# Places of a batch's rows: a segmented scan on VectorE and two products in place of seven products

## The chip, the cores and the metric

The kernel runs on one core of a Trainium2 chip. The metric is the device time of one execution in microseconds (us). The engines are TensorE (PE; its weight loads are shown as PEld), VectorE (DVE), ScalarE (ACT), GpSimd (POOL) and SyncE (SP, which here issues most of the DMAs). All data are float32.

## The reference

The kernel joins two blocks: an attention in which each query keeps its 32 best keys, and a mixture of experts in which each row goes to one expert.

```python
# attention: q, k, v are (8, 8, 576, 64)
scores = q @ k^T / 8
kth    = the 32nd largest score of each row
attn   = softmax(where(scores >= kth, scores, -1e9))
x      = (attn @ v), laid out as (4608, 512)      # one row per batch and position

# mixture of experts: w_gate (512, 8), w1 (8, 512, 1024), w2 (8, 1024, 512)
logits     = x @ w_gate
expert_idx = argmax(logits, axis=1)
gate_w     = softmax(logits)[row, expert_idx]
perm       = argsort(expert_idx, kind="stable")    # rows sorted by expert
for e in range(8):
    y_sorted[lo:hi] = relu(x_sorted[lo:hi] @ w1[e]) @ w2[e]
out = gate_w[:, None] * y
```

The change concerns the sorting: each row needs its place in a table in HBM (`x_rows`), in which expert e owns the places from e*CAP on, with CAP = 4736, in the order of arrival. A row's place is the first free place of its expert plus the number of earlier rows of the same batch that chose that expert.

## The kernel before

**Stages.** A loop of 144 steps covers 8 batches of 18 steps. Each step searches two tiles of 128 queries by 576 keys for their 32nd largest score. A batch has four units, each a pair of heads. At the end of a batch the gate logits of its 576 rows are complete, the rows get their places and are scattered to `x_rows` by indirect DMAs from GpSimd. From the second batch on, blocks of 128 rows of one expert, which are complete by then, go through the two products of the experts. These blocks are cut into 16 "pieces", which are put between the attention's products on TensorE. After the loop, the last batch is finished, and the remaining blocks run by themselves.

**The order on each engine** is the order in which the program is written, for TensorE, ScalarE and VectorE; nothing rearranges it. Each step of the loop writes:

- VectorE: `fold` (`h`, L315, and `l`, L316, from the scores `s`), `fold_on` (`few`, L322, and `hl`, L330; in the earlier part of the loop `hl` is made by GpSimd, L327 and L328), MAX8 and MATCH_REPLACE8 for the search (L351, L374, L385).
- ScalarE: `low` (L396), two activations `w` (L412), copies of scores from PSUM (`s`, L306), copies `wT` (L445, L447), two exponentials (L429), `wTt` (L462, L464), evacuations of the experts' products (L862, L976, L997).
- GpSimd: two subtractions on `w` (L421), 128x576 each, which wait for the two activations of L412; then `doubt` (L402), `nbias` (L380), scatters (L593) and stores (L880).
- TensorE: transposes `wTm` (L440) of the step before, which `wT` copies; expert pieces (`ph`, L971, and `py`, L988); scores of a later step (L299); output products `po` (L477) and `px` (L488).

Scores are made three steps ahead of their search.

**The end of a batch** is the generator `ending`. It runs over several steps of the loop: at each named place ("products", "small", "relu", "pool" and so on) it goes one stage on. For the sorting the stages are:

- `choice` (L530): five steps on VectorE make `oh`, the one-hot choice of each row (128 rows x 5 tiles x 8 experts), by L538 to L548. Tile 4 has only 64 rows; the upper half of its partitions is kept at zero by `e_same`.
- `ranks` (L554): seven products on TensorE into one PSUM bank `rank`. The first spreads `run`, the first free place of each expert, by the identity; the second multiplies by a triangle (`before`) and counts earlier rows in a tile; the other five multiply by `ones` and add the counts of earlier tiles. Columns 0 to 39 are the places, columns 40 to 47 the new `run`.
- `places` (L566): VectorE multiplies places and choice (L573), adds up (L578) and prepares the gate weights.
- ScalarE copies the new `run` out of PSUM (L1151), and `blocks` (L1153).
- `table` (L623) computes on VectorE, with few elements, which blocks are full (L645 and the lines after it); `filled_up` does so after batch 0, `counted` and `end_table` after the last.

The VectorE steps of `choice`, `places` and `table` don't run in one go. They are put into a list (`aside`), and the search takes one at each "tick". A search has six ticks, one behind each MAX8 and MATCH_REPLACE8 of its third and fourth round; a tick that finds a list at its end goes on to the next list, and does nothing if there is none. What is left of `choice` is taken at the place "turn", and `ranks` comes at "products", both in the following step. In the last batch there are no searches left, and all steps run one after the other.

`k.small` is a pool with two buffers for each name.

Of the kernel before, what the change touches and what calls it, by code (L numbers as in the profile page):

```python
# [9 lines left out]
F32 = mybir.dt.float32  # L10
I32 = mybir.dt.int32
AF = mybir.ActivationFunctionType
# [32 lines left out]
def kernel(  # L45
# [173 lines left out]
    wT = const.tile([P, NC, 2, S + ST], F32, name="wT")  # L219
    doubt = const.tile([P, B * U, NT, NL], F32, name="doubt")  # L220
    nc.gpsimd.memset(doubt, NEG)
    run = const.tile([P, E], F32, name="run")
    prepared.append(lambda: nc.vector.tensor_copy(run, e_at))
    rest_i = const.tile([1, 1], I32, name="rest_i")
    slot_last = const.tile([1, 2, NSLOT + SOON], I32, name="slot_last")
    slot_long = const.tile([1, 3, LONGS], I32, name="slot_long")
# [303 lines left out]
    def choice(lg):  # L530

        r = SimpleNamespace(lg=lg)
        mx = k.small.tile([P, KC], F32, name="mx")
        r.oh = oh = k.small.tile([P, KC, E], F32, name="oh")
        idx = k.small.tile([P, KC], F32, name="idx")

        def steps():
            nc.vector.tensor_reduce(mx, lg, axis=AX.X, op=ALU.max)  # L538
            yield
            nc.vector.tensor_tensor(lg, lg, _inner(mx[:, :], E), op=ALU.subtract)  # L540
            yield
            nc.vector.scalar_tensor_tensor(
                out=oh, in0=lg, scalar=0.0, in1=_ins(e_less[:, :], 1, KC), op0=ALU.is_ge, op1=ALU.mult
            )
            yield
            nc.vector.tensor_reduce(idx, oh, axis=AX.X, op=ALU.min)
            yield
            nc.vector.tensor_tensor(oh, e_same, _inner(idx[:, :], E), op=ALU.is_equal)  # L548
            yield

        r.steps = steps()
        return r

    def ranks(r):  # L554

        rp = bank("rank")
        ohf = r.oh[:, :, :].rearrange("p t e -> p (t e)")
        r.pos, r.run = rp[:, 0:KC * E], rp[:, KC * E:(KC + 1) * E]
        nc.tensor.matmul(rp[:, 0:(KC + 1) * E], ident, _ins(run[:, :], 1, KC + 1), start=True, stop=False)
        nc.tensor.matmul(r.pos, before, ohf, start=False, stop=False)  # L560
        for i in range(1, KC + 1):
            nc.tensor.matmul(
                rp[:, i * E:(KC + 1) * E], ones, ohf[:, 0:(KC + 1 - i) * E], start=False, stop=(i == KC)
            )

    def places(r, x):  # L566

        pos = k.small.tile([P, KC, E], F32, name="pos")
        r.posi = k.small.tile([P, KC], I32, name="posi")
        den = k.small.tile([P, KC], F32, name="den")  # L570

        def steps():
            nc.vector.tensor_tensor(pos, r.pos.rearrange("p (t e) -> p t e", e=E), r.oh, op=ALU.mult)  # L573
            yield
            nc.vector.tensor_reduce(den, r.lg, axis=AX.X, op=ALU.add)
            yield
            with nc.allow_low_precision(reason="one whole number and zeros are added"):
                nc.vector.tensor_reduce(r.posi, pos, axis=AX.X, op=ALU.add)  # L578
            yield
            nc.vector.tensor_scalar_add(den, den, EPS)  # L580
            yield
            nc.vector.reciprocal(x[:, :, Dm], den)
            yield

        return steps()
# [22 lines left out]
    def fill_up():  # L608

        ends = k.small.tile([1, E], I32, name="ends")  # L610
        nc.vector.tensor_copy(ends, run[0:1, :])
        for e in range(E):
            on = nc.gpsimd if e % 2 else nc.sync
            r = on.value_load(ends[0:1, e:e + 1], min_val=e * CAP, max_val=e * CAP + N)
            put = on.dma_start(x_rows[bass.ds(r, P), :], blank).ins
            if not k.exact:
                for other in scattered:
                    tc.add_manual_dep(put, other.name, WAIT)
                for other in fetched:
                    tc.declare_no_dep(put, other, reason="empty rows go behind all full blocks")  # L620
                fills.append(put)

    def table(slot_i, n, last, riding=None):  # L623
# [12 lines left out]
        def steps():  # L636
            if last:
                v.tensor_scalar(full, run[0:1, :], float(P - 1), 1.0 / P, ALU.add, ALU.mult)
                yield
                v.tensor_scalar(full, full, UNDER, WHOLE, ALU.add, ALU.add)  # L640
                yield
                for whole in (full, done):
                    v.tensor_scalar_add(whole, whole, -WHOLE)
            else:
                v.tensor_scalar(full, blocks, WHOLE, None, ALU.add)  # L645
            yield
            if riding is not None:
                v.tensor_tensor(full, full, riding, op=ALU.subtract)
                v.tensor_tensor(full, full, done, op=ALU.max)
                yield  # L650
            v.tensor_tensor(left, full, done, op=ALU.subtract)
            yield
            v.tensor_tensor_scan(upto[:, 1:], ones[0:1, 0:E], left, 0.0, op0=ALU.mult, op1=ALU.add)
            yield
            v.tensor_tensor(step[:, 0:E - 1], done[:, 1:E], full[:, 0:E - 1], op=ALU.subtract)
            yield
            v.tensor_tensor(first, _inner(slots[:, 0:n], E), _ins(upto[:, 1:], 1, n), op=ALU.is_ge)
            yield
            if last:
                v.tensor_reduce(slot_f[:, 0, 0:n], first, axis=AX.X, op=ALU.add)  # L660
                yield
            v.tensor_tensor(second, first, _ins(step[:, :], 1, n), op=ALU.mult)
            yield
            v.tensor_reduce(slot_f[:, 1, 0:n] if last else slot_f[:, :, 0:n], both, axis=AX.X, op=ALU.add)
            yield
            v.scalar_tensor_tensor(
                out=slot_f[:, 1, 0:n], in0=slot_f[:, 1, 0:n], scalar=done[:, 0:1], in1=at[:, 0:n],
                op0=ALU.add, op1=ALU.add,
            )
            yield  # L670
            v.tensor_tensor(slot_i[:, :, 0:n], slot_f[:, :, 0:n], _inner(slot_max[:, 0:2], n), op=ALU.min)
            yield
            if last:
                v.tensor_copy(rest_i, upto[:, E:])
            else:
                v.tensor_scalar_min(upto, upto, float(n))
                yield
                v.tensor_tensor(left, upto[:, 1:], upto[:, 0:E], op=ALU.subtract)
                yield
                v.tensor_tensor(done, done, left, op=ALU.add)  # L680
                yield

        return steps()

    def filled_up():

        most, few = k.small.tile([P, E], F32, name="left"), k.small.tile([P, E], F32, name="full")
        nc.vector.tensor_tensor(few, run, e_at, op=ALU.subtract)
        yield
        nc.vector.max(out=most, in_=few)  # L690
        yield
        nc.vector.scalar_tensor_tensor(
            out=few, in0=few, scalar=most[:, SOON - 1:SOON], in1=e_up, op0=ALU.is_ge, op1=ALU.mult
        )
        yield
        nc.vector.tensor_tensor(run, run, few, op=ALU.max)
        yield
        nc.vector.tensor_scalar(blocks, run[0:1, :], 1.0 / P, UNDER, ALU.mult, ALU.add)
        yield

    def counted():
# [3 lines left out]
        half, brief = wTt[0:1, 0:E], wTt[0:1, 8 * E + NSLOT + 3 * LONGS:9 * E + NSLOT + 3 * LONGS]  # L705
        up = k.small.tile([1, E], F32, name="left")
        for to, more in ((half, P - 1), (full, ST - 1), (up, P - FEW - 1)):
            nc.vector.tensor_scalar_add(to, run[0:1, :], float(more))
            nc.vector.tensor_copy(ci, to)
            nc.vector.tensor_single_scalar(ci, ci, 7, op=ALU.arith_shift_right)  # L710
            nc.vector.tensor_copy(to, ci)
# [304 lines left out]
    with fast:  # L1016
# [86 lines left out]
        def ending(b, u):  # L1103
# [46 lines left out]
            yield "relu"  # L1150
            nc.scalar.copy(run, r.run)  # L1151
            if b:
                nc.scalar.activation(blocks, r.run[0:1, :], AF.Copy, scale=1.0 / P, bias=UNDER)  # L1153
            yield "pool"
            through(steps)
            scatters.extend(scattering(r, x))
# [193 lines left out]
    with ExitStack() as outer:  # L1350
# [10 lines left out]
        with ExitStack() as st:  # L1361
# [1 line left out]
            open_pools(st, True)  # L1363
            ids = keep.tile([P, KC], I32, name="ids")
            token_ids(ids, 0)
            nc.vector.tensor_copy(run, e_at)
# [99 lines left out]
```

## Time and profile before

| | |
|---|---|
| Median of three runs | 1289.2 us (1288.89 to 1290.52) |
| The profiled execution, its time | 1292.85 us |
| Its span, first to last instruction | 1291.2 us |
| Mean granted clock of TensorE | 0.97 |
| Busy: TensorE, VectorE, ScalarE, GpSimd | 1182.6, 1064.5, 933.7, 729.8 us |
| Start of `rank` (L559) in the eight batches | 172.3, 303.7, 433.8, 565.8, 700.6, 834.2, 969.3, 1073.6 us |
| Last search ends | about 1054 us |

The busy share of an engine is an average over stages. A TensorE product of float32 shows as two instructions (two passes), each with its weight load. An engine's instruction can be stretched by a wait inside it and then counts as busy, so a full row isn't yet proof that the engine sets the pace. Matmul ends are modelled.

### The profile page before, as it was taken

The numbers are of one execution on the slowest core, as the hardware profiler recorded it, in microseconds if no ns is written. First come the engines' busy times: TensorE is split into PE (matmuls) and PEld (weight loads), VectorE is DVE, ScalarE is ACT, GpSimd is POOL, SyncE is SP. The second block draws the span as 40 slices with busy tenths as digits, with TensorE's granted clock in tenths as the row PEclk, the third lists the DMA queues.
The fourth block names the chain that finished last, engine by engine and source line by source line (L and its number), as shares of the span: only waits on it lengthen the run. The fifth ranks groups of instructions, "written<-read, shape, count | busy, mean of one in ns | idle before, by whom it ended". The sixth has DMA issues, their size and how long they took to land. (4 is left out here: it accounts for less than half of the span.)

```text
span 1291.2 us, 24609 instructions
## 1 busy us (share of the span) xinstructions
PE 1182.6 (92%) x7654; PEld 831.0 (64%) x7654; DVE 1064.5 (82%) x4600; ACT 933.7 (72%) x2136; POOL 729.8 (57%) x881
## 2 busy tenths in 40 slices
PE   6667767899889999999999999999999999999998
PEld 3444444666666566666667666666667667689975
DVE  8999999999999999999999999999999965000000
ACT  4888887888899888888788888888887872112121
POOL 4777776786778665658555855666557643000010
PEclk9888888999999999999999999999999999999999
DMA  5010113641374138533946464537455548996682
GB/s 152 31 30 31 31 39 115 260 167 39 122 266 166 39 128 310 185 122 103 337 131 215 161 230 157 186 134 264 175 177 202 170 148 281 341 367 234 214 296 86
DMA packets 98702, 220.82 MB, mean 171 GB/s; under 512 B 5309, under 2 KB 26301, under 8 KB 98560
## 3 DMA queue, kind: packets, MB, share of 16 engines
q1 hardware_dynamic: 91360, 198.87, 44.8%
q0 software_dynamic: 6384, 19.97, 4.3%
q8 instruction: 62, 1.02, 0.3%
q14 instruction: 80, 0.66, 0.2%
q10 hardware_dynamic: 816, 0.31, 0.1%
HBM read 195.75 MB, written 24.04 MB: 170 GB/s over the span
## 5 line engine op out<-in xcount | busy, mean ns | idle before, releaser
L421 POOL TENSOR_TENSOR w<-s,w 128x576 f32<-128x576 f32 x288 | 408.4, 1439 | 325.8 <-ACT w L412 325.6
L971 PE MATMUL ph<-xTs,w 128*128 128x128 f32 x2112 | 262.9, 278 | 3.8 <-ACT xTs L862 2.6
L971 PEld LDWEIGHTS ph<-xTs,w 128*128 128x128 f32 x2112 | 251.1, 194 | 22.4 <-issue 17.6
L988 PE MATMUL py<-w,hT 128*128 128x512 f32 x528 | 249.7, 602 | 1.9 <-ACT hT L976 1.6
L429 ACT ACTIVATE w<-w,nbias 128x576 f32<-128x576 f32 x288 | 223.1, 785 | 1.9 <-POOL w L421 0.9
L440 PE MATMUL wTm<-turn,w 128*128 128x128 f32 x1152 | 172.4, 289 | 52.3 <-ACT oT L479 31.4
L412 ACT ACTIVATE w<-s,low 128x576 f32<-128x576 f32 x288 | 207.6, 768 | 4.7
L299 PE MATMUL sc<-qkb 64*128 64x288 f32 (+1 forms) x1280 | 198.8, 462 | 8.3 <-DMA qkb<-in_qk_dram 4.2
L440 PEld LDWEIGHTS wTm<-turn,w 128*128 128x128 f32 x1152 | 134.2, 147 | 109.4 <-ACT oT L479 38.1
L306 ACT COPY s<-sc 128x576 f32<-128x576 f32 x288 | 168.0, 634 | 12.9 <-PE sc L299 12.9
L447 ACT COPY wT<-wTm 128x512 f32<-128x512 f32 x256 | 140.7, 596 | 37.1 <-PE wTm L440 36.4
L374 DVE MAX8 tops<-scr 128x8 f32<-128x168 f32 x576 | 164.8, 313 | 0.0
L299 PEld LDWEIGHTS sc<-qkb 64*128 64x128 f32 (+1 forms) x1280 | 106.9, 190 | 71.9 <-issue 35.9
L374 DVE MAX8 tops<-few 128x8 f32<-128x144 f32 (+1 forms) x576 | 150.8, 299 | 0.0
L988 PEld LDWEIGHTS py<-w,hT 128*128 128x128 f32 x528 | 92.2, 192 | 87.1 <-issue 83.7
L477 PE MATMUL po<-wT,vb 128*64 128x288 f32 x1024 | 144.6, 427 | 0.0
L880 POOL DMA_INDIRECT out_dram<-y,xg x37 | 39.0, 1054 | 161.3 <-ACT y L997 85.0
L351 DVE MAX8 few<-l 128x8 f32<-128x288 f32 x288 | 126.7, 440 | 0.0
L315 DVE TENSOR_TENSOR h<-s 128x576 f32<-128x576 f32 (+1 forms) x145 | 111.1, 766 | 4.3 <-ACT s L306 4.0
L477 PEld LDWEIGHTS po<-wT,vb 128*64 128x64 f32 x1024 | 70.3, 142 | 68.4 <-issue 17.5
L316 DVE TENSOR_TENSOR l<-s 128x576 f32<-128x576 f32 (+1 forms) x145 | 112.5, 776 | 0.0
L351 DVE MAX8 few<-hl 128x8 f32<-128x72 f32 x576 | 99.1, 209 | 0.0
(203 smaller groups left out, 1593.0 us busy)
## 6 DMA issues: line engine op xcount, KB each, us to landing
w<-in_moe_w_dram SPq DMA_DIRECT2D x74, 2048.0 KB
qkb<-in_qk_dram SPq DMA_DIRECT2D x31, 608.0 KB
vb<-in_v_dram SPq DMA_DIRECT2D x32, 320.0 KB
xg<-x_rows SPq DMA_DIRECT2D x37, 257.0 KB
x_rows<-blank SPq DMA_DIRECT2D x13, 257.0 KB
x_rows<-blank POOLq DMA_DIRECT2D x4, 257.0 KB
x_rows<-x,posi POOLq DMA_INDIRECT x40, 3.2
out_dram<-y,xg POOLq DMA_INDIRECT x37, 4.6
```

The source lines that it names most:

```text
L299: nc.tensor.matmul(ps[rows, j, 0:HF], n.q[d, cols], n.k[d, keys], start=True, stop=True)
L306: lambda m=m, ps=ps: nc.scalar.copy(s[:, m, :, :], ps[:, :, 0:HF]) for m, ps in enumerate(got)
L351: nc.vector.max(out=f.few[:, m, QF + 8 * j:QF + 8 * j + 8], in_=away)
L374: nc.vector.max(out=tops[:, m, r * 8:(r + 1) * 8], in_=src[m])
L412: nc.scalar.activation(w[:, m, :], s[:, m, :, :].rearrange("p j k -> p (j k)"), AF.Relu, scale=-STEEP, bias=low[:, m:m + 1],)
L421: k.last_pool = in_turn(nc.gpsimd.tensor_tensor(w[:, m, :], s[:, m, :, :].rearrange("p j k -> p (j k)"), w[:, m, :], op=ALU.subtract)).ins
L429: nc.scalar.activation(w[:, m, :], w[:, m, :], AF.Exp, scale=scale, bias=nbias[:, m:m + 1], accum_out=n.z[:, c:c + 1])
L440: nc.tensor.transpose(pm[:, c * P:(c + 1) * P], w[:, m, first:first + P], ident)
L447: nc.scalar.copy(wT[:, :, m, q], pm4)
L477: nc.tensor.matmul(po[r, 0:HF], n.v[:, c, r], rhs, start=(c == 0), stop=(c == KC - 1))
L971: nc.tensor.matmul(ph[:, f, :], n.w1[:, 0, dt, fc * P:(fc + 1) * P], n.xT[:, dt, :], start=(dt == 0), stop=(dt == DT - 1),)
L988: nc.tensor.matmul(py, hT[:, f, :], n.w2[:, 0, f, :], start=(f == 0), stop=(f == FT - 1))
```

## The change

A constant tile `chosen` of 128 partitions x 8 experts x 6 columns holds in its columns 1 to 5 the one-hot choice of the five tiles, and in column 0, on partition 0 alone, `run`. A second constant tile `anew` is 0 in column 0 and 1 elsewhere. A scan on VectorE, state = anew * state + chosen, starts anew with each expert and gives on each partition the sums over the tiles so far, `run` included on partition 0. One product with `ones` adds these over the partitions, which gives `run` plus the counts of earlier tiles, and one product with the triangle adds the earlier rows of the tile. The last column of each expert is the new `run`, of which only row 0 is read. `run` thus exists on one partition. Two tiles of `k.small` (`oh`, `pos`) have one buffer in place of two, and `places` takes the buffer of `oh`. On GpSimd three memsets are added at the start.

```diff
-    run = const.tile([P, E], F32, name="run")
-    prepared.append(lambda: nc.vector.tensor_copy(run, e_at))
+    chosen = const.tile([P, E, KC + 1], F32, name="chosen")
+    run = chosen[0:1, :, 0]
+    anew = const.tile([P, E, KC + 1], F32, name="anew")
+    nc.gpsimd.memset(chosen, 0.0)
+    nc.gpsimd.memset(anew, 1.0)
+    nc.gpsimd.memset(anew[:, :, 0], 0.0)
+    prepared.append(lambda: nc.vector.tensor_copy(run, e_at[0:1, :]))
...
     def choice(lg):
         r = SimpleNamespace(lg=lg)
+        r.oh = chosen[:, :, 1:].rearrange("p e t -> p t e")
+        r.upto = k.small.tile([P, E, KC + 1], F32, name="pos", bufs=1)
         mx = k.small.tile([P, KC], F32, name="mx")
-        r.oh = oh = k.small.tile([P, KC, E], F32, name="oh")
+        oh = k.small.tile([P, KC, E], F32, name="oh", bufs=1)
...
-            nc.vector.tensor_tensor(oh, e_same, _inner(idx[:, :], E), op=ALU.is_equal)
+            nc.vector.tensor_tensor(r.oh, e_same, _inner(idx[:, :], E), op=ALU.is_equal)
+            yield
+            one, other, to = (a[:, :, :].rearrange("p e t -> p (e t)") for a in (anew, chosen, r.upto))
+            nc.vector.tensor_tensor_scan(to, one, other, 0.0, op0=ALU.mult, op1=ALU.add)
             yield
...
     def ranks(r):
         rp = bank("rank")
-        ohf = r.oh[:, :, :].rearrange("p t e -> p (t e)")
-        r.pos, r.run = rp[:, 0:KC * E], rp[:, KC * E:(KC + 1) * E]
-        nc.tensor.matmul(rp[:, 0:(KC + 1) * E], ident, _ins(run[:, :], 1, KC + 1), start=True, stop=False)
-        nc.tensor.matmul(r.pos, before, ohf, start=False, stop=False)
-        for i in range(1, KC + 1):
-            nc.tensor.matmul(
-                rp[:, i * E:(KC + 1) * E], ones, ohf[:, 0:(KC + 1 - i) * E], start=False, stop=(i == KC)
-            )
+        n = E * (KC + 1)
+        r.pos, r.run = rp[:, 0:n].rearrange("p (e t) -> p t e", e=E), rp[0:1, KC:n:KC + 1]
+        nc.tensor.matmul(rp[:, 0:n], ones, r.upto[:, :, :].rearrange("p e t -> p (e t)"), start=True, stop=False)
+        nc.tensor.matmul(
+            rp[:, 0:n - 1], before, chosen[:, :, :].rearrange("p e t -> p (e t)")[:, 1:], start=False, stop=True
+        )
...
     def places(r, x):
-        pos = k.small.tile([P, KC, E], F32, name="pos")
+        pos = k.small.tile([P, KC, E], F32, name="oh", bufs=1)
...
-            nc.vector.tensor_tensor(pos, r.pos.rearrange("p (t e) -> p t e", e=E), r.oh, op=ALU.mult)
+            nc.vector.tensor_tensor(pos, r.pos[:, 0:KC, :], r.oh, op=ALU.mult)
...
     def filled_up():
-        most, few = k.small.tile([P, E], F32, name="left"), k.small.tile([P, E], F32, name="full")
-        nc.vector.tensor_tensor(few, run, e_at, op=ALU.subtract)
+        most, few = k.small.tile([1, E], F32, name="left"), k.small.tile([1, E], F32, name="full")
+        nc.vector.tensor_tensor(few, run, e_at[0:1, :], op=ALU.subtract)
```

Where `run[0:1, :]` was read (in `fill_up`, `table`, `counted`, `filled_up`), `run` is read now, and `blocks` is made from `r.run` in place of `r.run[0:1, :]`. The order of all other instructions on each engine stays.

More of the change, by code (lines that the diff above doesn't have):

```diff
@@ L610, in fill_up @@
         ends = k.small.tile([1, E], I32, name="ends")
-        nc.vector.tensor_copy(ends, run[0:1, :])
+        nc.vector.tensor_copy(ends, run)
         for e in range(E):
@@ L637, in steps @@
             if last:
-                v.tensor_scalar(full, run[0:1, :], float(P - 1), 1.0 / P, ALU.add, ALU.mult)
+                v.tensor_scalar(full, run, float(P - 1), 1.0 / P, ALU.add, ALU.mult)
                 yield
@@ L692, in filled_up @@
         nc.vector.scalar_tensor_tensor(
-            out=few, in0=few, scalar=most[:, SOON - 1:SOON], in1=e_up, op0=ALU.is_ge, op1=ALU.mult
+            out=few, in0=few, scalar=most[:, SOON - 1:SOON], in1=e_up[0:1, :], op0=ALU.is_ge, op1=ALU.mult
         )
@@ L697, in filled_up @@
         yield
-        nc.vector.tensor_scalar(blocks, run[0:1, :], 1.0 / P, UNDER, ALU.mult, ALU.add)
+        nc.vector.tensor_scalar(blocks, run, 1.0 / P, UNDER, ALU.mult, ALU.add)
         yield
@@ L707, in counted @@
         for to, more in ((half, P - 1), (full, ST - 1), (up, P - FEW - 1)):
-            nc.vector.tensor_scalar_add(to, run[0:1, :], float(more))
+            nc.vector.tensor_scalar_add(to, run, float(more))
             nc.vector.tensor_copy(ci, to)
@@ L1152, in ending @@
             if b:
-                nc.scalar.activation(blocks, r.run[0:1, :], AF.Copy, scale=1.0 / P, bias=UNDER)
+                nc.scalar.activation(blocks, r.run, AF.Copy, scale=1.0 / P, bias=UNDER)
             yield "pool"
@@ L1365 @@
             token_ids(ids, 0)
-            nc.vector.tensor_copy(run, e_at)
+            nc.vector.tensor_copy(run, e_at[0:1, :])
             nc.vector.tensor_scalar(done, e_at[0:1, :], 1.0 / P, WHOLE, ALU.mult, ALU.add)
```

## The prediction

> **What bounds the kernel now.** I began with the page: busy shares, then the 40 slices, to see which engine fills which part of the span.
>
> ```profile
> PE 1182.6 (92%) x7654; PEld 831.0 (64%) x7654; DVE 1064.5 (82%) x4600; ACT 933.7 (72%) x2136; POOL 729.8 (57%) x881
> PE   6667767899889999999999999999999999999998
> DVE  8999999999999999999999999999999965000000
> ```
>
> VectorE is full until about 1055 us and then empty; TensorE is at 6 to 7 tenths at first, at 9 or more from some 260 us, and alone in the last 230 us. Two full rows don't say which of them sets the pace, so next I took the waits of TensorE by stage: first 60 to 500 us, then 500 to 1060 us (columns: who waited for whom, us in total, times, longest).
>
> ```profile
> PE wTm L440 <- ACT oT L479: 31.4, 21, 4.5
> PE wTm L440 <- ACT xl L495: 16.3, 6, 3.1
> PE wTl L456 <- ACT wT L447: 14.0, 17, 2.6
> ...
> PE wTl L456 <- ACT wT L447: 5.2, 11, 1.1
> PE py L988 <- ACT hT L976: 1.6, 3, 0.6
> ```
>
> Up to 500 us TensorE stands 71 us in 440 waiting for others. After 500 us all its waits make 9.4 us in 560. So in the second stage it is TensorE that never rests. How can VectorE be full there too? From the timeline I took the starts of `h` (L315), one for each of the 144 searches. Early they are 6.55 us apart, later 6.92, but some gaps are 9.1 to 9.8. The timeline of one such search, after the products of batch 5, shows why (columns: start us, length us):
>
> ```profile
> 834.19 0.42 PE L559 MATMUL rank<-run,turn 128*128 128x48 f32 x2
> 835.77 5.40 PE L988 MATMUL py<-w,hT 128*128 128x512 f32 x12
> 841.01 1.04 PE L440 MATMUL wTm<-turn,w 128*128 128x128 f32 x8
> 841.64 1.08 ACT L445 COPY wT<-wTm 128x512 f32<-128x512 f32 x2 [3.70 <-PE wTm L440]
> ...
> 845.91 2.79 POOL L421 TENSOR_TENSOR w<-s,w 128x576 f32<-128x576 f32 x2 [6.92 <-ACT w L412]
> 846.00 1.35 DVE L645 TENSOR_SCALAR full<-blocks 1x8 f32<-1x8 f32 x1
> 847.52 1.20 DVE L651 TENSOR_TENSOR left<-full,done 1x8 f32<-1x8 f32 x1
> ```
>
> Read it downwards: TensorE works without a gap from `rank` to `wTm`, ScalarE stands 3.70 us for `wTm`, so its `low` and `w` of the next tiles come late, so GpSimd's two subtractions (L421, 1.4 us each) come late and fall on VectorE's small steps. L645 and L651 do 8 elements, 0.14 us where nothing is in the way; here they last until a subtraction ends. VectorE's "busy" hides a wait for a late TensorE. Batches 3 to 6 are 132 to 135 us apart (L559 to L559), while 18 searches of 6.92 us and some 2.5 us of small steps make 127: 5 to 8 us of slack per batch. **TensorE bounds the kernel from about 500 us on, VectorE before.**
>
> **What the Trainium skill says.** "SBUF — State Buffer", section "Who interferes with whom": a VectorE instruction with two SBUF inputs contends with a GpSimd instruction that reads SBUF, and the one that began first keeps the pair of ports to its end. The trace agrees (L651: 1.20 us beside L421, 0.14 elsewhere). "DVE: opcode table, instruction layouts, handler registers and perf-mode slots", section 6, "Datapath and trigger behaviour": `tensor_tensor_scan` runs at half throughput. Only scans of 1x8 are in this trace (0.16 to 0.17 us, against 0.15 for a plain 1x8 step), too small to show it. "TensorE: Matmul & The Clock Gate", section "Back-to-back issue gap": the spacing of products is set by weight load and product together. The trace agrees: the ten passes of L562, with 40 down to 8 columns, follow each other evenly, so fewer columns save nothing and a whole product does.
>
> **The change, part by part.**
>
> *TensorE.* Each product is two passes (x16 in eight batches). In batch 6 the seven products start at 969.27 us and the next work at 970.85: 1.58 us. L559 takes 969.27 to 969.53 (0.26), L560 to 969.74 (0.21), the five of L562 the other 1.11. What stays is two products of 48 and 47 columns: 0.26 + 0.23 = 0.49. Saved: **1.09 us a batch.** Their waits: they need the scan, which ends with its search, 5 us or more ahead of `rank` in seven batches.
>
> *VectorE.* One scan of 128x48 more in each batch, after the last MAX8 of the search and before `h`. A 1x8 scan holds the engine 0.09 us (1079.50 to the next start at 1079.59); 40 elements more cost 40 x 0.8 ns (a 128x40 step 0.174, a 1x8 step 0.148: 0.8 ns each), twice that at half throughput, 0.07 us: **0.16 us.** Low end 0.12 (full rate), high end 0.3 (3.5 ns an element, if the whole excess of the 1x8 scan over a plain step were due to its elements). If it met L421 it would last up to 1.4 us longer; but at its seven places (behind L548 at 166.7, 294.9, 423.7, 555.2, 691.6, 826.4 and 959.4 us) no subtraction runs, the next starts 1.2 us or more after. Seven scans: 1.1 us, bounds 0.8 to 2.1. The tick that it takes was an empty one.
>
> *Edits at nothing.* `oh` and `pos` are now written and read in strides of six: nothing, at most 0.03 us each (their 32 extra elements twice). `run` on one partition instead of 128: the same 0.15 us, the length was not in the partitions. Three memsets on GpSimd at the start, two of 128x48 and a small one: at most 0.14 us each (the row of `rz`), 0.4 us. Behind them wait `blank`, SP's nine x_rows issues, and VectorE's casts, which already last until GpSimd is done (4.1 us); VectorE then idles 1.57 us before `h` at 6.68, and SP issues no load until 22.7. If that cover were gone, 0.4 us. VectorE's first copy of `run` now waits for one of these memsets, done before the casts end. ScalarE's copy of `run` waits for the scan too, which precedes the product that it waits for anyway. SP and the DMAs issue the same things in the same order.
>
> *What reaches the end.* In the five searches like the one shown, I moved ScalarE's chain earlier by as much as it stood waiting for TensorE (1.09 at most), VectorE's steps later by 0.16, and asked where L421 then ends. Batch 5: from 845.91 to 844.85; L645 at 846.16 meets only the end of the first half, L651 the second: 1.05 us of stall in place of 2.25, gain 1.2. The same for batch 6 gives 0.85, batch 4 0.98 (L421 is over before L645), batch 3 0.77. Sum 3.8, of at most 4 x 1.09 = 4.4. In batches 1 and 2, where TensorE bounds only in places, the same reading of L645 and L651 gives 0.65 and 0.8; I take 1.4. Batch 0: TensorE waits for ScalarE right after (2.85 us), nothing.
>
> *The last batch*, where nothing is searched any more:
>
> ```profile
> 1073.51 0.20 DVE L548 TENSOR_TENSOR oh<-e_same,idx 128x40 f32<-128x40 f32 x1
> 1073.56 0.32 PE L559 MATMUL rank<-run,turn 128*128 128x48 f32 x2
> 1075.12 2.03 PE L971 MATMUL ph<-xTs,w 128*128 128x128 f32 x16
> ```
>
> TensorE used to begin with `run` while `oh` was finishing; now it waits for `oh` (1073.71) and for the scan (0.3 alone), until about 1074.05, and ends at 1074.55 instead of 1075.1: 0.5 us gained, though the scan lies on the path.
>
> Sum: -3.8 - 1.4 + 1.1 - 0.5 = **-4.6 us.** Taking all scans as lengthening is cautious, since after 500 us they lie beside TensorE's work. The profiled execution took 1292.85 us (span 1291.2), 3.65 above the median of 1289.2; so 1288.2 against its own time, and 1284.6 as a median.
>
> **The rivals.**
>
> 1. *TensorE's freed time comes through* (the forecast): 1281 to 1286.6. For it: 9.4 us of waits in 560. Against: a search gains or loses in steps of 1.4 us. Chance 0.66.
> 2. *VectorE sets the pace throughout*, freed time only makes TensorE wait longer for ScalarE: +1.1 - 0.5 = +0.6, so 1289.8. For it: VectorE's full row, and that `h` waited for `s` only 4.0 us in all. Against: the long gaps. With a part of the gain coming through it reaches down to 1286.6. Chance 0.20.
> 3. *Slower: the lead turns into more collisions.* L322 and L330, the folds, normally just miss L421; where they meet it whole (L322 at 956.37 lasts 1.30 us, L330 1.65, together 2.1 more than their 0.44 each) a search costs 2.1 to 2.6 us. Moving ScalarE and VectorE against each other by a microsecond changes who meets whom in the searches that follow. From four new meetings the gain is gone and 3.8 to 5.8 lost: 1293 to 1295. Against: lateness of L421 makes them, and the change lessens it. Chance 0.14.
>
> That the products aren't fewer is excluded: they are written out in `ranks`.
>
> **How the numbers follow.** About 0.2%, 2.6 us, is what a measurement of this kernel can tell from no change: faster is below 1286.6, slower above 1291.8. The likeliest case gives 1284.6. Low end: all eight batches at 1.09 would give -8.7; I take 1281.0. High end: rival 2 with scans at 0.3 gives 1290.8, and one new meeting leads to 1291.5. Some 0.07 is left out below, 0.13 above.
>
> **What would show it.** Rank passes 32 instead of 112 over the kernel; from the first product to the next work 0.5 us, not 1.58; a scan of 128x48 that holds VectorE 0.12 to 0.3 us; gaps of `h` two searches after `rank` shorter than now in batches 2 to 6 (9.27, 8.23, 8.36, 9.66, 9.51); L559's successor in batch 6 earlier than 969.3 by some 3 us, and in batch 2 not by more than 1. I'm wrong if TensorE's waits after 500 us rise by 4 us or more (rival 2), or if L322 and L330 grow by 8 us in all (rival 3).

## The result, and the profile after

| | before | after |
|---|---|---|
| Median, 5 runs each on one chip | 1289.07 us (1288.09 to 1290.52) | 1283.32 us (1282.36 to 1284.61) |
| Ratio | | 0.995, 95% interval 0.9939 to 0.9961 |
| The profiled execution, its time and span | 1292.85, 1291.2 us | 1284.61, 1283.0 us |

The changed kernel is faster by 5.75 us; the forecast was 4.6. Run again on another chip (e9 below) it came to 1283.61 us beside 1290.71 for the kernel before, 7.1 us less, ratio 0.994 (0.9926 to 0.9954). From here on line numbers are those of the changed kernel: `h` L320, `l` L321, `few` L327, `w` L417, the subtractions L426, `wTm` L445, the scan L558, the two products L569 and L570, the table's first small steps L653 and L659 (before: L645 and L651).

First the page again, the busy row and the two slice rows:

```profile
PE 1176.1 (92%) x7574; PEld 823.6 (64%) x7574; DVE 1058.8 (83%) x4608; ACT 933.3 (73%) x2136; POOL 732.0 (57%) x884
PE   6767767898899999999999999999999999999998
DVE  8999999999999999999999999999999965000000
```

TensorE does 80 passes less (7654 to 7574), VectorE 8 instructions more, and VectorE is nevertheless busy for 5.7 us *less*. That can't be work: the scans add 1.9 us. About 3 of the 5.7 us are chance of the profiled execution of before: e1 below, with the seven products and a scan, shows 1061.4 us. The rest is stretched time that has gone. The slices look as before; a change of half a per cent isn't seen in them. The groups by form show the new operations and the small steps (columns: number, busy us and mean ns of one, idle us before them):

```profile
L659 DVE TENSOR_TENSOR left<-full,done 1x8 f32<-1x8 f32 x8 | 3.2, 397 | 0.0
L653 DVE TENSOR_SCALAR full<-blocks 1x8 f32<-1x8 f32 x8 | 2.7, 341 | 0.0
L558 DVE TENSOR_TENSOR_SCAN pos<-anew,chosen 128x48 f32<-128x48 f32 x8 | 1.9, 240 | 0.0
L570 PE MATMUL rank<-chosen,before 128*128 128x47 f32 x16 | 3.1, 281 | 0.0
```

L653 and L659 together fell from 10.1 us (706 and 549 ns, eight of each) to 5.9. They do the same 8 elements. The timeline after the products of batch 5 shows where (the same stretch of work as shown for the kernel before):

```profile
829.96 0.42 PE L569 MATMUL rank<-pos,ones 128*128 128x48 f32 x2
830.22 0.39 PE L570 MATMUL rank<-chosen,before 128*128 128x47 f32 x2
830.43 5.40 PE L996 MATMUL py<-w,hT 128*128 128x512 f32 x12
835.66 1.04 PE L445 MATMUL wTm<-turn,w 128*128 128x128 f32 x8
836.30 1.07 ACT L450 COPY wT<-wTm 128x512 f32<-128x512 f32 x2 [2.59 <-PE wTm L445]
...
840.56 2.78 POOL L426 TENSOR_TENSOR w<-s,w 128x576 f32<-128x576 f32 x2 [5.80 <-ACT w L417]
841.90 0.14 DVE L653 TENSOR_SCALAR full<-blocks 1x8 f32<-1x8 f32 x1
842.21 1.15 DVE L659 TENSOR_TENSOR left<-full,done 1x8 f32<-1x8 f32 x1
```

Count from the first product. `py` begins 0.47 us after it, before it was 1.58. ScalarE stood 2.59 us for `wTm` instead of 3.70, 1.11 less. The subtractions begin at 10.60 instead of 11.72, 1.12 earlier; VectorE's L653 begins at 11.94 instead of 11.81, 0.13 later. So it slips past the first subtraction, and only L659 is held, to the end of the second: 1.29 us for both instead of 2.55.

The waits of TensorE after 500 us (who for whom, us in total, times, longest), of which the two largest:

```profile
PE wTl L461 <- ACT wT L452: 5.2, 11, 1.1
PE py L996 <- ACT hT L984: 1.6, 3, 0.6
```

They are as before, and all lines together make 9.7 us where 9.4 were seen before. TensorE used the freed time; it didn't wait it away.

### The profile page after: what moved, and what is told of

Read it like the earlier page. It is cut to its first block, busy times and chain, and to the rows that moved or that the text cites. A ratio compares the mean times of both kernels' runs of the same rounds, so it can differ in the third digit from the quotient of the medians.

```text
span 1283.0 us, 24461 instructions
## 1 busy us (share of the span) xinstructions
PE 1176.1 (92%) x7574; PEld 823.6 (64%) x7574; DVE 1058.8 (83%) x4608; ACT 933.3 (73%) x2136; POOL 732.0 (57%) x884
## 5 line engine op out<-in xcount | busy, mean ns | idle before, releaser
L426 POOL TENSOR_TENSOR w<-s,w 128x576 f32<-128x576 f32 x288 | 409.2, 1441 | 317.5 <-ACT w L417 317.4
L445 PE MATMUL wTm<-turn,w 128*128 128x128 f32 x1152 | 173.9, 291 | 52.7 <-ACT oT L484 29.1
L417 ACT ACTIVATE w<-s,low 128x576 f32<-128x576 f32 x288 | 207.7, 768 | 4.7
L445 PEld LDWEIGHTS wTm<-turn,w 128*128 128x128 f32 x1152 | 135.1, 148 | 111.6 <-ACT oT L484 35.5
L379 DVE MAX8 tops<-scr 128x8 f32<-128x168 f32 x576 | 169.5, 328 | 0.0
L379 DVE MAX8 tops<-few 128x8 f32<-128x144 f32 (+1 forms) x576 | 154.9, 314 | 0.0
L356 DVE MAX8 few<-l 128x8 f32<-128x288 f32 x288 | 129.8, 451 | 0.0
L320 DVE TENSOR_TENSOR h<-s 128x576 f32<-128x576 f32 (+1 forms) x145 | 111.7, 770 | 3.9 <-ACT s L311 3.6
L321 DVE TENSOR_TENSOR l<-s 128x576 f32<-128x576 f32 (+1 forms) x145 | 114.3, 788 | 0.0
L356 DVE MAX8 few<-hl 128x8 f32<-128x72 f32 x576 | 102.3, 221 | 0.0
```

The costliest lines, as they stand in the source:

```text
L356: nc.vector.max(out=f.few[:, m, QF + 8 * j:QF + 8 * j + 8], in_=away)
L379: nc.vector.max(out=tops[:, m, r * 8:(r + 1) * 8], in_=src[m])
L417: nc.scalar.activation(w[:, m, :], s[:, m, :, :].rearrange("p j k -> p (j k)"), AF.Relu, scale=-STEEP, bias=low[:, m:m + 1],)
L426: k.last_pool = in_turn(nc.gpsimd.tensor_tensor(w[:, m, :], s[:, m, :, :].rearrange("p j k -> p (j k)"), w[:, m, :], op=ALU.subtract)).ins
L445: nc.tensor.transpose(pm[:, c * P:(c + 1) * P], w[:, m, first:first + P], ident)
```

## The experiments

Theory T is the forecast: TensorE sets the pace after 500 us, its freed time comes through, VectorE's added time is hidden there. The other theories are named in the expectations. Three groups of kernels ran, each on one chip with the kernel before: there 1292.19 us (e1 to e4), 1291.62 (e5 to e8) and 1290.71 (e9 to e12). Differences are between medians of one group; a ratio's interval is 0.0009 to 0.0015 to each side, 1.1 to 1.9 us. The expectations of e1 to e8 name times on the level of the first comparison (before at 1289.07 us); on the level of their own group these times lie 3.1 us (e1 to e4) and 2.6 us (e5 to e8) higher.

### Scan without its use, and products put back: e1 to e4

e1 is the kernel before with a scan of 128x48 at the place where the change has it, its result unused (the diff is shortened; `oh` and `pos` also get one buffer in place of two):

```diff
+            one = ones[:, 0:E * (KC + 1)]
+            nc.vector.tensor_tensor_scan(summed, one, one, 0.0, op0=ALU.mult, op1=ALU.add)
+            yield
```

> The kernel before, with its seven products, and a scan of 128x48 on VectorE (of constants, its result unused) at the place where the changed kernel has its own. Theory T (TensorE sets the pace from about 500 us on, VectorE before; the gain is TensorE's freed time): 7 x 0.12 to 0.16 us at most, less where TensorE sets the pace: 1289.4 to 1290.2, and the long gaps of h two searches after rank are those of the kernel before (9.3, 8.2, 8.4, 9.7, 9.5 us in batches 2 to 6). Rival R (the gain comes from the scan shifting VectorE's steps against GpSimd's): about 1284.

Measured: 1290.71 us, ratio 0.9991 (0.998 to 1.0002). The interval reaches from 2.6 us faster to 0.3 slower. So the scan alone doesn't give the 0.995, and it costs less than T said (1292.5 to 1293.3 on this group's level). The long gaps of batches 2 to 6 stay near those of before, as T expected (9.13, 8.23, 8.19, 9.45 and 9.36 us).

e2, e3 and e4 are the changed kernel with five products of 40 to 8 columns, into unused columns of the same bank, ahead of the two: in all batches, in batches 3 to 6, in batches 0 to 2 (shortened: `batches` stands for the list, `upto` for `r.upto` laid flat).

```diff
+        if r.b in batches:
+            for i in range(1, KC + 1):
+                nc.tensor.matmul(rp[:, SM // 2:SM // 2 + (KC + 1 - i) * E], ones, upto[:, 0:(KC + 1 - i) * E], start=True, stop=True)
```

> The changed kernel, with five more products by ones (40, 32, 24, 16 and 8 columns, into columns of the bank that nobody reads) ahead of its two in all eight batches: TensorE's load is that of before, all else is that of after. T: the gain goes wholly and the scan remains as a cost, and in the last batch the scan now delays seven products: 1289.5 to 1290.8. R (scan or shift): 1283.3. A third theory, S (the gain comes from the start and from what the other edits do there): 1283.3 too.

Measured: 1291.64 us, ratio 0.9997 (0.9988 to 1.0006). From the first product to the next work it is again 1.58 us. With the five products back the gain is gone, although the scan, the new buffers and the memsets at the start are all still there. The interval leaves at most 1.6 us for everything else in the change, so at least some 4 of the 5.75 us are the products'.

> The changed kernel, with the same five products in batches 3 to 6 alone, where TensorE hardly waits. T: four times up to 1.09 us come back: 1286.7 to 1287.7. R and S: 1283.3.

Measured: 1289.18 us, ratio 0.9981 (0.9972 to 0.9989). On this group's level T said 1289.8 to 1290.8, R and S 1286.4: T is nearer, and e3 lies 0.6 us below its band.

> The changed kernel, with the same five products in batches 0 to 2 alone, where TensorE waits 70 us in 440. T: batch 0 nothing, batches 1 and 2 up to 1.25 us each: 1283.3 to 1285.5, and the gap of h two searches after rank in batch 2 back from 8.0 to about 9.3 us. If instead every freed us of TensorE counts everywhere: 1286.6.

Measured: 1286.4 us, ratio 0.9961 (0.9946 to 0.9976), at the lower end of T's band (1286.4 to 1288.6 on this level). The gap of batch 2 came to 8.75 us here and to 9.10 in e2, where 9.3 was expected.

Taking the products out of batches 3 to 6 and of the last batch (e2 to e4) brings 5.2 us; out of batches 0 to 2 and of the last (e2 to e3) 2.5. If the last batch counts for 1.1 in each (in the traces, 1.55 us from the first product to the next work with the five, 0.44 without), that is 4.1 us for the four late batches, 1.0 each of the 1.09 that TensorE saves, and 1.4 for the three early ones, under 0.5 each. By the scatter of the runs these shares are good to some 0.3 us a batch. That the late batches count for more is clear from e3 and e4 alone: they differ by 2.8 us, where equal shares, four batches against three, would make a difference of one batch.

Where in a batch does it sit? The gaps between starts of `h` in e1 and in e7 (below: also a scan, but two products; another chip) differ by more than 0.3 us at few places. One search, between the first and the second `h` after `rank`, is shorter in batches 2 to 6 by 0.83, 0.84, 0.82, 0.79 and 0.71, and one near the end of the loop by 0.41; e3, set against e7, takes back 0.82, 0.83, 0.82 and 0.71 in batches 3 to 6 and 0.45 near the end. In batch 1 it is 8.00 us in e1 and 8.02 in e7: nothing. The timeline of e1 in that search of batch 5, and then of e7:

```profile
842.87 1.14 DVE L649 TENSOR_SCALAR full<-blocks 1x8 f32<-1x8 f32 x1
844.18 1.19 DVE L655 TENSOR_TENSOR left<-full,done 1x8 f32<-1x8 f32 x1
```

```profile
839.92 1.42 DVE L653 TENSOR_SCALAR full<-blocks 1x8 f32<-1x8 f32 x1
841.50 0.14 DVE L659 TENSOR_TENSOR left<-full,done 1x8 f32<-1x8 f32 x1
```

Seven products: both small steps last until a subtraction ends, they are held. Two products: one. Whether it is the first or the second that stays held differs between executions.

### The dose on VectorE behind the scan: e5 and e6

Three MAX8 of 128x320 on constant data more, right behind the scan, in batches 3 to 6 (e5) or 0 to 2 (e6) (shortened: `batches` stands for the list):

```diff
             nc.vector.tensor_tensor_scan(to, one, other, 0.0, op0=ALU.mult, op1=ALU.add)
+            if r.b in batches:
+                for _ in range(3):
+                    nc.vector.max(out=oh[:, 0, :], in_=turn[:, :, :].rearrange("p a b -> p (a b)"))
```

> The changed kernel, with three MAX8 of 128x320 (1.1 us of VectorE in all, results unused, no contention with GpSimd) behind the scan in batches 3 to 6: four times 1.1 us of VectorE where T says that TensorE sets the pace. T: under a third of the 4.4 us reaches the end: 1283.3 to 1284.8; the gaps of h at the scan grow by 1.1 us and later gaps of the same batch shrink. If VectorE sets the pace: 1287.7.

> The same three MAX8 in batches 0 to 2, where T says that VectorE sets the pace: 3 x 1.1 us reach the end, 1286.0 to 1286.6. If TensorE set the pace there too: about 1283.5.

Measured: e5 1291.12 us, ratio 0.9994 (0.9985 to 1.0003); e6 1296.27 us, ratio 1.0035 (1.0022 to 1.0048). Against e7 of the same group that is 8.3 and 13.5 us slower. **Both expectations of T missed**, and not by a little; e5 is even beyond the number of the other theory (1290.2 on this group's level). Two things were wrong with the experiment. The dose was undersized: it holds VectorE 1.44 us a time, not 1.1, so 5.8 us in e5 and 4.3 in e6. And the place was bad, as the timeline of e6 in batch 0 shows:

```profile
166.48 1.52 DVE L561 MAX8 oh<-turn 128x8 f32<-128x320 f32 x3
167.92 1.62 DVE L320 TENSOR_TENSOR h<-s 128x576 f32<-128x576 f32 x1
169.46 1.97 DVE L321 TENSOR_TENSOR l<-s 128x576 f32<-128x576 f32 x1
...
167.52 3.30 POOL L426 TENSOR_TENSOR w<-s,w 128x576 f32<-128x576 f32 x2 [2.17 <-ACT w L417]
```

`h` and `l` normally take 0.73 and 0.75 us and are nearly over when the subtractions begin, since those follow the last MAX8 by `low` and `w` on ScalarE. The dose stands between the last MAX8 and `h`, so it pushes `h` and `l` onto the subtractions, where they take 1.62 and 1.97. The search with the scan grows by 1.43 us (7.86 to 9.29), the next by 2.55 (6.54 to 9.09). In e5 the same happens in batches 4 to 6 (9.70 to 11.14 and 6.92 to 9.21 in batch 4; in batch 3 the next search falls by 1.0 instead), and 1.3 of it comes back two searches after `rank` in batches 5 and 6. TensorE's waits from 500 to 1060 us rise from 10.0 us (e7) to 15.4: with `h` and `l` on the subtractions, TensorE does wait. 3.9 us of them are a single wait in batch 4, for VectorE to read `rank` out of a PSUM buffer that TensorE needs next (explained at e11 below); in e6 the same wait comes to 4.4 us in batch 1 (1.25 without a dose) and 3.1 in batch 2. That is part of why the cost exceeds the dose. The two kernels say what a step at this place costs, not which engine sets the pace in the changed kernel.

### Triangle first, and the table later: e7 and e8

e7 issues the triangle product ahead of the one that needs the scan (`chosen` gets one more column so that both write 48; `mx` gets one buffer in place of two). e8 takes the small steps of the table one search later in batches 1 to 6. In the first edit `upto` and `flat` stand for `r.upto` and `chosen` laid flat:

```diff
-        nc.tensor.matmul(rp[:, 0:n], ones, upto, start=True, stop=False)
-        nc.tensor.matmul(rp[:, 0:n - 1], before, flat[:, 1:], start=False, stop=True)
+        nc.tensor.matmul(rp[:, 0:n], before, flat[:, 1:n + 1], start=True, stop=False)
+        nc.tensor.matmul(rp[:, 0:n], ones, upto, start=False, stop=True)
```

> The changed kernel with its two products in the other order: the product with the triangle, which needs only the choice, is first, so that in the last batch it runs beside the scan. T: 0.2 us less in the last batch (rank to the next work 0.5 us, beginning at the end of the choice), nothing elsewhere: 1283.1, not to be told from 1283.3. If the scan's place on the path in the last batch counted for more: below 1282.5.

Measured: 1282.81 us, ratio 0.9928 (0.9916 to 0.9941). In the last batch the time from the start of the choice (L555, in e7 L556) to the next `ph` falls from 1.10 us to 0.84, as expected. The whole is lower than expected: on this group's level T said 1285.7, and the other reading, that the scan's place counts for more, began below 1285.1. That doesn't decide for the other reading: the changed kernel isn't in this group, and it was 5.75 us below the kernel before in one group and 7.1 in another. Whether more than 0.26 of e7's 8.8 us comes from the order of the products stays open.

```diff
                     steps = table(slot_i, new, False)
+                    if b:
+                        yield "weights"
+                        yield "pool"
                 aside.append(steps)
```

> The changed kernel, in which the small VectorE steps of table are put into the list one search later in batches 1 to 6, so that they don't fall on GpSimd's late subtractions after rank. T (these stalls of VectorE are how a late TensorE shows, not a cost of their own): the stalls go (some 3 us of them) and the end moves by under 1 us: 1282.5 to 1284.3. If the stalls themselves set the end: about 1280.5. If the later loads of blocks leave TensorE without work: slower, with waits of TensorE for weights or rows in the loop.

Measured: 1281.96 us, ratio 0.9921 (0.9909 to 0.9934), 0.85 below e7. The runs of the two overlap (1279.72 to 1283.84 and 1282.06 to 1283.70), so the times don't tell T's gain of under 1 us from the nearly 3 of the other reading. TensorE's waits from 500 to 1060 us stay at 9.8 us (e7: 10.0), so the later loads don't leave it without work. The group by form of e8 shows that L659 is now free of any subtraction:

```profile
L659 DVE TENSOR_TENSOR left<-full,done 1x8 f32<-1x8 f32 x8 | 1.1, 139 | 0.0
```

L653 isn't: its eight make 2.9 us, against 4.5 in e7, and it is held in batches 5 and 6 (0.75 and 0.83 us). The searches two after `rank` fall in batches 2 to 6 by 4.7 us in all (8.30 to 6.98, 7.39 to 6.87, 7.37 to 6.88, 8.66 to 7.33, 8.65 to 7.62). But the ones after them grow (in batch 5 by 0.35 and 0.84), and over the whole loop, with 1.1 us saved in batch 1, only 2.1 us are left between the two traces. Part of what is given back is simply the moved steps: in batches 3 and 4, where neither small step is held in e7 (0.14 us each), one search falls by 0.5 us and a later one grows by 0.9 and 0.55. So the giving back is no proof that TensorE sets the pace.

### The dose again at another place: e9 to e12

e9 is the changed kernel unchanged, for comparison. e11 and e12 have e5's and e6's three MAX8 behind `l` of the following search, so that `h` and `l` stay where they were (the diff is shortened; `choice` sets `k.dose` behind the scan in the batches named).

```diff
+            if getattr(k, "dose", None) is not None:
+                for _ in range(3):
+                    nc.vector.max(out=k.dose, in_=turn[:, :, :].rearrange("p a b -> p (a b)"))
+                k.dose = None
             if not f.aside:
                 lists(f)
```

> The changed kernel as it is, on the chip of the next three, so that each of them can be set against it and not only against the kernel before. Both theories: 0.995 of the kernel before (0.9939 to 0.9961).

> Three more MAX8 of 128x320 (1.1 us of VectorE) in batches 3 to 6, not behind the scan as in e5 but one place later, behind `l` of the next search, so that `h` and `l` keep their distance to the search before and are not pushed onto GpSimd's subtractions. T (TensorE bounds after 500 us, VectorE has slack there): most of the 4.4 us is hidden, 0 to 1.5 us slower than e9, TensorE's waits after 500 us stay under 11. V (VectorE sets the pace there too, and e5 showed that rightly): 4.4 us or more slower than e9, waits of TensorE after 500 us up by 4 or more.

Measured: e9 1283.61 us, ratio 0.994 (0.9926 to 0.9954); e11 1285.65 us, ratio 0.9958 (0.9944 to 0.9971), 2.0 us slower; all five runs lie below 1288.0, where V's band begins. TensorE's waits from 500 to 1060 us are 11.7 us (e9: 10.0), a little over T's 11, and up by 1.7 where V wanted 4. The dose is 5.8 us, not the 4.4 of the expectation; about a third of it comes through. T's band ended at 1.5, V's began at 4.4: T is nearer, but its number too was missed. The searches show what became of each dose: in batch 3, 0.4 us come through; in batch 4 all 1.45, and nothing comes back; in batches 5 and 6 the search of the dose grows by 1.46, and two later 1.28 and 1.16 are given back. Batch 5 of e9, then of e11:

```profile
841.99 1.42 DVE L653 TENSOR_SCALAR full<-blocks 1x8 f32<-1x8 f32 x1
843.57 0.14 DVE L659 TENSOR_TENSOR left<-full,done 1x8 f32<-1x8 f32 x1
```

```profile
845.35 0.14 DVE L659 TENSOR_SCALAR full<-blocks 1x8 f32<-1x8 f32 x1
845.66 0.14 DVE L665 TENSOR_TENSOR left<-full,done 1x8 f32<-1x8 f32 x1
```

VectorE comes 3.36 us later to the small steps (line numbers of e11 are 6 higher), 1.90 of which it brought along from earlier batches. TensorE comes to `rank` 1.91 us later (830.00 to 831.91) and to `px` behind it 2.07 (846.57 to 848.64): it hardly notices the dose. The subtractions therefore end before the small steps, nothing is held, and VectorE is back at 2.1 us. In such a batch VectorE has room, and TensorE decides.

Batch 4 is different. There e9, and then e11, have behind `rank`:

```profile
700.78 0.65 PE L445 MATMUL wTm<-turn,w 128*128 128x128 f32 x4 [0.15 <-DVE oh L581]
```

```profile
702.72 0.66 PE L449 MATMUL wTm<-turn,w 128*128 128x128 f32 x4 [1.61 <-DVE oh L587]
```

TensorE stands for `oh`, here VectorE's product of places and choice, which reads `rank`. In the kernel `rank` and `wTm` take turns in the same two PSUM buffers (`ps_t`), so this half of `wTm` can't begin until VectorE has read `rank`. The wait is 0.15 us without the dose and 1.61 with it; in batch 3 the same wait comes to 0.49. These two waits together are about the 2.0 us that e11 loses. So T's "VectorE has slack there" holds in batches 5 and 6, holds for two thirds of the dose in batch 3, and fails in batch 4, where VectorE sets the pace as soon as it is given work.

> The same three MAX8 behind `l`, in batches 0 to 2. T: VectorE bounds here, so the 3.3 us come through, 2.3 to 4 us slower than e9. If e6's 13.5 us came from the place (h and l pushed onto the subtractions) and not from VectorE being dear in general, this one stays at or below 4. If VectorE's lateness is paid several times over wherever it arises: 8 us or more.

Measured: 1291.68 us, ratio 1.0009 (1.0 to 1.0018), 8.1 us slower than e9 for 4.3 us added. Missed as well: T said 4 at most, and the number of the other reading, 8 us or more, came true. The place explains 5.4 of e6's 13.5 us (e6 against e7, e12 against e9), not all that is over. In the trace of e12 the three searches with the dose grow by 1.88, 1.45 and 1.44, together 4.8. Where the rest arises, the two traces don't tell. Of the 8.4 us by which their last `h` are apart, 0.9 come before the first dose. Another 1.6 are in two searches at the start of batch 1, in the second of which `h` and `l` meet the subtractions:

```profile
198.16 1.56 DVE L320 TENSOR_TENSOR h<-s 128x576 f32<-128x576 f32 x1
199.65 1.95 DVE L321 TENSOR_TENSOR l<-s 128x576 f32<-128x576 f32 x1
```

In e9 `h` of this search takes 0.73 there and only `l` is held. This search is 9.44 us long in e12, 8.46 in e9 and 7.65 in e7. But the kernel before, which has no dose, is 9.44 us long there too, with `h` at 1.56 and `l` at 1.96 us. That an added microsecond before 500 us costs nearly two is measured by the medians; which of the meetings belong to the dose and which would have come in any execution is not settled.

> The triangle product ahead of the ones product (e7) and the table's steps one search later (e8) together. If the two act at different places (e7 frees TensorE a little earlier where it used to wait for the scan, e8 takes VectorE's small steps out of the subtractions' way) their gains add: e7 was 0.2 us or less, e8 about 1 us better than the changed kernel, so 0.8 to 1.5 us faster than e9. If they draw on the same slack, no more than e8 alone: about 1 us or less.

e10 has e7's and e8's edits together. Measured: 1282.17 us, ratio 0.9927 (0.9914 to 0.9941), 1.4 us below e9. That is within the 0.8 to 1.5 expected of gains that add, but its interval overlaps that of e9, so it isn't shown that it beats the changed kernel; against the kernel before it is 0.7% faster. Its profiled execution (span 1283.2 us) was slower than its median, so the trace doesn't place the 1.4 us.

## Why the prediction was right, point by point

The path was right: TensorE's shorter `rank` lets ScalarE and GpSimd come earlier, and VectorE's small steps are held for less. Some terms of the sum were not right: the scans' cost, batch 1, and VectorE's slack in batch 4. That it came close is partly luck, as said below.

- **What bounds.** Right for what TensorE saves: by e2 to e4 about 1.0 us of every 1.09 us of TensorE comes through in the late stage, and TensorE's waits from 500 to 1060 us stay at 9.7 us. Too broad for VectorE: the 5 to 8 us of slack a batch were not there in batch 4, where e11 passes on all 1.45 us. In that batch time taken from TensorE and time added to VectorE both count, so the bold sentence "TensorE bounds the kernel from about 500 us on" is only part of the truth.
- **1.09 us a batch.** 1.58 us became 0.47 in batches 1 to 6. Right.
- **The scan.** It lasts 0.24 us, but delays what follows by less: the search with it grew by 0.14 to 0.21 us in the seven batches, 1.2 in all (predicted 0.16 and 1.1). One reading was off: of the seven 1x8 scans in the loop before, six last 0.15 us and one, held by a subtraction, 1.14; 0.16 to 0.17 us are those behind the loop. What failed is the step "taking all scans as lengthening": in e1 scans of the same size at the same place move the kernel by -2.6 to +0.3 us. The 1.1 us is a term that the end doesn't show.
- **The reading of the held steps.** Batch 5 was worked out as 1.06 us earlier for the subtractions and 0.16 later for VectorE, gain 1.2. The trace has 1.12, 0.13 and 1.27. The gaps two searches after `rank` went from 9.27, 8.23, 8.36, 9.66, 9.51 to 8.02, 7.38, 7.35, 8.39, 8.69: gains of 1.25, 0.85, 1.01, 1.27 and 0.82 in batches 2 to 6, against 0.8, 0.77, 0.98, 1.2 and 0.85 predicted. Between e1 and e7 they are smaller, 0.71 to 0.84, since which of the two steps is held differs by execution.
- **Batch 1** was to gain 0.65 and gained nothing (8.01 to 8.02 us). The forecast moved ScalarE and GpSimd earlier by what TensorE saves. The second pair of subtractions behind `rank` began 8.56 us after it before and 8.58 after, because TensorE waited the saved time away. In batch 1, before and then after:

```profile
307.12 1.37 PE L440 MATMUL wTm<-turn,w 128*128 128x128 f32 x8
```

```profile
304.82 0.66 PE L445 MATMUL wTm<-turn,w 128*128 128x128 f32 x4 [1.25 <-DVE oh L581]
```

VectorE reads `rank` 3.87 us after the first product in both kernels, and the second half of `wTm` needs the buffer. With seven products (before, e1, e2, e4) this wait isn't there in batch 1; with two (after, e3, e5, e7 to e11) it is 1.24 to 1.26 us. The sum left this wait out. In batch 2 the same wait, 1.24 us, is there in the profiled executions of e9 and e10 and absent in those of after and e7. A search near the end of the loop, which had been given nothing, gained 0.35 to 0.41.
- **The last batch.** 0.5 us predicted; from the start of the last output products (`px`) to the first `ph` behind `rank` 6.79 became 6.27 us, 0.52:

```profile
1067.06 0.23 DVE L555 TENSOR_TENSOR chosen<-e_same,idx 128x40 f32<-128x40 f32 x1
1067.32 0.26 DVE L558 TENSOR_TENSOR_SCAN pos<-anew,chosen 128x48 f32<-128x48 f32 x1
...
1067.72 0.39 PE L569 MATMUL rank<-pos,ones 128*128 128x48 f32 x2 [0.45 <-DVE pos L558]
1067.95 0.39 PE L570 MATMUL rank<-chosen,before 128*128 128x47 f32 x2
1068.16 2.03 PE L979 MATMUL ph<-xTs,w 128*128 128x128 f32 x16
```

TensorE stands 0.45 us for the scan, and is still earlier.

- **The sum.** -4.6 against -5.75. The searches and the last batch gain 4.9 us between e1 and e7 (predicted 5.7), so that step was some 0.8 too large, and the scans, put at +1.1, cost nothing that the runs can tell. The two misses offset: that is luck. The 4.9 us of the traces and the 5.75 and 7.1 of the medians agree only within the noise.
- **A sign that read wrong.** In batch 2 `rank` was to come at most 1 us earlier, and came 3.3 earlier (433.80 to 430.53); in batch 6 it came 5.4 earlier instead of 3 (969.27 to 963.89). About 3 us of this arise in batches 0 and 1, in searches where nothing of the change shows. e1, with seven products, is ahead of the kernel before by the same 3 us there: the profiled execution of before was slow in them by chance. That is also why the profiled pair differs by 8.2 us and the medians by 5.75.
- **The rivals.** "VectorE sets the pace throughout" falls with the result itself (1289.8 us and 4 us more of TensorE's waits were its signs) and with e2 to e4. In batch 1 it is right: TensorE's freed time becomes a wait, though for VectorE and not, as it said, for ScalarE. For batch 4, and for the first 500 us, where VectorE's added time costs nearly double, it also saw something that the forecast left out. "The lead turns into more collisions" would have needed L322 and L330 to grow by 8 us; their counterparts L327 and L335 grew by 2.8 (78.4 to 80.2 and 50.1 to 51.1). Nearly all of that is some 0.01 us on each of the 251 instructions; those more than 0.1 us above their median are 24 and 2 in number, 23 and 2 before, so there were no new meetings to speak of. e5 and e6 show that the mechanism exists, at up to 2.6 us a search, with a shift of 1.44 us; the change shifts VectorE by 0.15.

## What to carry to other kernels

Where an engine is full but some of its 8-element steps last a microsecond, read what those steps are held by and follow it back; here it led from VectorE over GpSimd and ScalarE to TensorE, and the gain could be read from one timeline. Work added to a full engine was priced here by where it pushed the steps behind it, not by its own length: the same three MAX8 cost 8.3 us behind the scan and 2.0 us one place later. Time freed on one engine comes through only up to the next buffer that another engine has to give back: here that was `rank`, and it took the whole gain of batch 1. And before a microsecond is explained from two profiled executions, a third one, here that of a kernel that should change nothing, tells which of it is chance.

## What the runs showed of the hardware

- A plain TENSOR_SCALAR of 1x8 (L653, one tensor input) is held by GpSimd's subtraction as a two-input step is: 1.42 us beside it, 0.14 without. The prediction read L645 so, but gave only the rule for two inputs. The same section of the Trainium skill ("SBUF — State Buffer", section "Who interferes with whom") also says that `tensor_scalar` can take both ports for its one input and can then contend with GpSimd; the 1.42 us agree with that.
- Held time is counted as busy: from e1 to e7, both with eight scans, VectorE showed 3.2 us less busy time (1061.4 to 1058.2) for the same steps.
- A float32 product's two passes take about the same whether 8 or 48 columns are written: ten passes of 40 down to 8 columns last 1.1 us from first start to the next work, 0.11 each; two passes of 48 or 47, 0.21 to 0.26.
- A scan of 128x48 lasts 0.24 us on average, one of 1x8 0.154 (L661): 2.1 ns for each of 40 elements more, against the 0.8 of a plain step, 2.6 times as much. The half throughput that the prediction took from the Trainium skill ("DVE: opcode table, instruction layouts, handler registers and perf-mode slots", section 6) is in that direction; the two durations alone don't show whether it is exactly half.
